# Whole stores for the last batch, and unread matmuls from the gather of batch 1 on, in a fused attention and mixture-of-depths kernel

## The chip, the cores and the metric

One core of a Trainium2 chip runs the kernel. The metric is device time in microseconds; the kernel before was run three times.

## The reference

Four batches of `x[6208, 256]` go through a cross-covariance attention over channels, and then through a mixture of depths that works on 128 tokens of each batch. Cut to what matters:

```python
qn = q / (norm(q, axis=1) + 1e-6)
kn = k / (norm(k, axis=1) + 1e-6)
a = softmax(kn.transpose(0, 2, 1) @ qn / tau)
x = v @ a

scores = x @ w_gate
out = x.copy()
for b in range(B):
    top = the 128 tokens of batch b with the largest scores
    xe = x[b, top]
    ye = relu(xe @ w1) @ w2
    out[b, top] = xe + sigmoid(scores[b, top])[:, None] * ye
```

q, k, v and out are float32, 25.4 MB each.

## The kernel before, in words

A batch is cut into six full chunks of 1024 rows and a remainder of 64 rows. In a full chunk each of the 128 partitions holds 8 neighbouring rows, so a partition's share of an output chunk is 8 KB of contiguous memory, and the chunk is 1 MB.

**Loads.** `emit_load` (L238, L240) issues the loads on POOL, which casts them to bf16 on the way: for each batch first q and k of all chunks, then v. `pump` emits them as far ahead as buffers and a limit of bytes in flight allow. In the model they share one ring (0), the stores another (1).

**First pass.** `p1_row` (L380 to L384) multiplies each row group of q and k into the sums of q-k products and of the norms, in PSUM. One chunk is 16 groups of three matmuls. `softmax_stages` makes the attention matrix of the batch from them.

**Second pass.** `p2_transpose` (L484) transposes v, `p2_score` (L529) makes the scores, `p2_out` (L563) multiplies by the attention matrix, and ScalarE copies the result to a staging tile (L574). When a chunk's staging tile is full, `out_store` calls `emit_store` (L586; L588 for the remainder), which issues the store on SP.

**Selection and the mixture of depths.** `select_stages` searches the threshold of the 128 largest scores, makes the indices, gathers the tokens' rows of v (L716, on POOL), and multiplies them by the attention matrix and by w1 and w2 (L740 to L800). `upd` (L804) is the result, and L818 scatters it into the output, on POOL, when every store of that batch has landed.

**The last batches.** L is batch 3 and E is batch 2. The stores of batches 2 and 3 wait until the last load, GATE, has landed. The last two chunks of batch 2 (`late`) are computed after all of batch 3, with the update added by matmuls (L570), so that the scatter of batch 2 need not wait for their stores; they are stored last of all. The scatter of batch 3 waits for the stores of batch 3 and not for those two. A full chunk of batch 3 is stored in two halves, partitions 0 to 63 and 64 to 127, issued one behind the other when the chunk is complete; all other chunks are stored whole.

**The order.** A loop at the end of the kernel writes the instructions in the order that a model gives: `Engines` holds a clock for each engine, `Rings` one for the transfers, and among the steps that are ready the loop takes the one of the smallest priority: chains of softmax and selection (0), scores (1), first pass and transposes (2), outputs (3). The model of PE knows two speeds, by how much PE did before. Where nothing is ready for more than FILL = 0.1 us, `unread` (L515) emits a matmul of constants into columns of the score bank that nobody reads; `cast_done`, true once the weights have been cast, allows it from early in batch 0 on. `gathered` is the set of batches whose gather has been emitted; with E = 2 it reaches that size at the gather of batch 1.

Of the kernel before, what the change touches and what calls it, by code (L numbers as in the profile page):

```python
# [17 lines left out]
P = 128  # L18
# [91 lines left out]
def kernel(  # L110
# [12 lines left out]
    nc = tc.nc  # L123
# [11 lines left out]
    NFULL = NL * CPL  # L135
# [34 lines left out]
    def lview(t, b, d):  # L170
        if d < NL:
            return t[b, d * LCH:(d + 1) * LCH, :].rearrange("(p s) c -> p s c", s=LR)
        return t[b, NL * LCH:N, :]

    def view(t, b, ci):
        if ci < NFULL:
            return lview(t, b, ci // CPL)[:, ci % CPL * RPP:(ci % CPL + 1) * RPP, :]
        return lview(t, b, NL)
# [4 lines left out]
    L = B - 1  # L183
    E = B - 2
# [8 lines left out]
    def late(b, ci):  # L193
        return b == E and ci in LATE
# [6 lines left out]
    def now():  # L201
        return eng.t["pe"]
# [49 lines left out]
    def pump():  # L252
        rings.run(now())
        flying[:] = [key for key in flying if rings.done.get(key, FAR) > now()]
        while nxt_unit[0] < len(units):
            u = units[nxt_unit[0]]
            if not slots[bucket(u)] or sum(length[key] for key in flying) >= AHEAD:
# [11 lines left out]
                      in_=moe_w1.rearrange("(dc p) f -> p dc f", p=P))  # L269
# [74 lines left out]
    gathered = set()  # L344
# [12 lines left out]
    def bank_free(kind):  # L357
        return banks[bank_pick(kind)][0]
# [154 lines left out]
    def unread():  # L513
        t = scores_of(sc_last[0])
        nc.tensor.matmul(t[:, 256:512], lhsT=ident_b, rhs=w1_sb[:, 0, 0:256], start=not sc_open[0],  # L515
                         stop=not sc_open[0])
        eng.pe(1, 256)
# [62 lines left out]
    def apart(later, earlier):  # L580
        tc.declare_no_dep(later.ins, earlier.ins, reason="rows of the last batch and of the batch before it")

    def emit_store(b, ci, lo, hi):
        st = stage_of[(b, ci)]
        if ci < NFULL:
            ins = nc.sync.dma_start(out=view(out, b, ci)[lo:hi], in_=st[lo:hi])  # L586
        else:
            ins = nc.sync.dma_start(out=view(out, b, ci), in_=st[:REM, 0, :])  # L588
        if late(b, ci):
            late_inst.append(ins)  # L590
            if L in scatter_inst:
                apart(ins, scatter_inst[L])
        return ins
# [278 lines left out]
    cast_done = False  # L872
    drained = False
    fill_at = [0.0]
    FILL = 0.1
# [3 lines left out]
    def stage_ready():  # L879
        if len(stage_keys) < ST_BUFS:  # L880
            return 0.0
        key = stage_keys[-ST_BUFS]
        if key in stage_free:
            return stage_free[key]
        return rings.landing(("st",) + key)

    def out_store(b, ci):
        dep = stage_done[(b, ci)]
        if b >= E and not gate_done:
            dep = max(dep, rings.landing(GATE))  # L890
        if late(b, ci):
            dep = max(dep, rings.landing(("scatter", E)))
        parts = (2 if b == L else 1) if ci < NFULL else 1
        for h in range(parts):
            key = ("st", b, ci) if h == parts - 1 else ("st", b, ci, h)
            issued = eng.issue("sp", 0.42, dep)
            rings.add(1, issued + 0.65, STORE / parts + 0.009 if ci < NFULL else 0.2, key, 0.45)
            ins = emit_store(b, ci, h * P // parts, (h + 1) * P // parts)
        stored[b].append(key)
        if not late(b, ci):  # L900
            held[b] -= 1
        return ins

    while True:
        pump()
        if not cast_done and now() > 8.0:
# [11 lines left out]
            cast_done = True  # L918
# [3 lines left out]
        if deferred and GATE in load_inst:  # L922
            for b, ci in deferred:
                st = out_store(b, ci)
                if not gate_done:
                    gate_done.append(1)
                    tc.add_manual_dep(
                        st.ins, load_inst[GATE].ins.name,
                        mybir.DependencyInfo(mybir.DependencyClass.Sync, mybir.DependencyReason.DATA),
                        reason="stores behind the last loads")  # L930
            deferred = []
        t = now()
# [3 lines left out]
        if eat_at < len(eat):  # L936
            kind, u, x = eat[eat_at]
            if u in loaded:
# [4 lines left out]
                r = rings.landing(arrival_key[u + (row,)]) + MARGIN  # L943
                if kind == "p1":
                    if u[2] == FIRST and x == 0:
                        r = max(r, acc_free[0])
                elif vt_slots or acc_dead[0] and u[2] < NL:
                    r = max(r, bank_free("vt"))
                else:
                    r = FAR  # L950
                able.append((r, 2, kind))
        if score_at < len(scores):
            b, g = scores[score_at]
            if b in aw_ready and (b, g) in vts:
                able.append((max(aw_ready[b], vt_ready[(b, g)]), 1, "S"))
        if out_at < len(outs):
            b, g, pr = outs[out_at]
            if b in a_ready and (b, g) in vts and score_at > gs.index(g) + b * len(gs):
                r = max(a_ready[b], vt_ready[(b, g)], bank_free("o"))
                if late(b, g[0]):  # L960
                    r = max(r, late_add[2] if E in scatter_inst else FAR)
                if g[0] < NFULL and g[1] == 0 and pr == 0:
                    r = max(r, stage_ready())
# [12 lines left out]
        if fit:  # L976
            r, prio, what = min(fit, key=lambda a: (a[1], a[0]))
        else:
            r, prio, what = min([a for a in able if a[0] > t], key=lambda a: (a[0], a[1]))
            if cast_done and r - t > FILL and t >= fill_at[0]:  # L980
                unread()
                fill_at[0] = now() + PAUSE
                continue
            if r - t > FILL and fill_at[0] > t:
                eng.t["pe"] = min(r, fill_at[0])
                continue
            eng.t["pe"] = max(t, r)
            t = now()
# [26 lines left out]
        elif what == "S":  # L1015
            b, g = scores[score_at]
            score_at += 1
            f = p2_score(b, g)
            if g == gs[-1]:
                chains.append(Chain(select_stages(b, f), b))  # L1020
        else:
            b, g, pr = outs[out_at]
            out_at += 1
            f = p2_out(b, g, pr)
            if out_at == len(outs) or outs[out_at][1] != g:
                vts.pop((b, g))
                if (b, g) in from_pool:
                    from_pool.discard((b, g))
                    vt_slots.append(f)
            if out_at == len(outs) or outs[out_at][1][0] != g[0]:  # L1030
                if b >= E and not gate_done:
                    deferred.append((b, g[0]))
                else:
                    out_store(b, g[0])
# [35 lines left out]
```

## Time and profile before

| what | us |
|---|---|
| median of 3 runs | 267.47 |
| lowest and highest | 266.99, 267.75 |
| the profiled execution | 267.31 |
| its span in the profile | 265.2 |
| PE busy | 231.5 (87%) |
| VectorE, ScalarE, POOL busy | 96.9, 100.4, 56.4 |
| chain that ended last: DMA, PE | 53%, 32% |

The profile comes from one execution, and times in it count from the start of its span. Busy time of PE overlaps itself, since matmuls are pipelined. PE is TensorE, DVE VectorE, ACT ScalarE, SP the engine that issues the stores, POOL GpSimd; L586 is line 586 of the kernel. "PEclk" is the share of TensorE's full clock that was granted. "[3.00 <-DMA x]" behind an instruction is the idle time of its engine before it and what ended most of it. Time to landing runs from a transfer's issue to its last byte.

### The profile page before, as it was taken

Reading aid. Unit: us, or ns where it says so; the run is one execution under the profiler, and the core shown is the slowest. Engines: PE = TensorE matmul, PEld = TensorE weight load, DVE = VectorE, ACT = ScalarE, POOL = GpSimd, SP = SyncE. Lnnn points to the kernel's source line nnn. Section 1 sums busy time; section 2 is a strip of 40 time slices with the busy share of each in tenths; the row PEclk is TensorE's granted clock in tenths of the full one; section 3 lists DMA queues with packets and bytes.
Section 4 is the critical chain, followed back from the end, with each engine's and each line's share of the span. In section 5 each row is a group of like instructions: output and inputs, shape, how many; then the busy total and the mean of one; then the engine's idle time right before and its main releaser. Section 6 shows DMA issues by size and latency. Waiting matters only on the chain.

```text
span 265.2 us, 7006 instructions
## 1 busy us (share of the span) xinstructions
PE 231.5 (87%) x3043; PEld 203.0 (77%) x3043; DVE 96.9 (37%) x410; ACT 100.4 (38%) x179; POOL 56.4 (21%) x105
## 2 busy tenths in 40 slices
PE   0099989999999979999999979999999989999660
PEld 0079878889889979798789969888989978787440
DVE  0100003567520013757630011747663287764030
ACT  3700004852830022854632002766122084597310
POOL 7223113212040105213021014133223300011001
PEclk9999999999999999999999999999999999999975
DMA  7999999999999999999999999999999997999994
GB/s 236 258 216 211 214 216 211 211 214 287 296 316 319 309 213 212 224 212 281 290 313 316 317 228 213 221 216 208 217 213 209 213 210 231 421 273 283 316 336 185
DMA packets 16847, 66.89 MB, mean 252 GB/s; under 512 B 2097, under 2 KB 3634, under 8 KB 13618
## 3 DMA queue, kind: packets, MB, share of 16 engines
q0 software_dynamic: 12528, 38.93, 73.6%
q1 hardware_dynamic: 4290, 27.53, 28.1%
q8 instruction: 23, 0.38, 0.5%
q14 instruction: 6, 0.05, 0.0%
HBM read 78.91 MB, written 25.95 MB: 395 GB/s over the span
## 4 chain that ended last, share of the span: by engine, by line
DMA 53%; PE 32%; issue 4%; DVE 3%; POOL 3%; ACT 1%; SPq 1%; POOLq 1%; DVEq 0%
DMA k_ch<-in_k_dram 39%; DMA v_ch<-in_v_dram 7%; PE s_ps L380 6%; PE o_ps L563 5%; DMA q_ch<-in_q_dram 5%; PE g_ps L384 3%; PE g_ps L382 3%; DMA out_dram<-stage 3%; PE vt_ps L484 3%; PE sc_ps L529 2%; PE sc_ps L515 1%; SPq L586 1%; PE g_ps L563 1%; PE m_ps L648 1%; PE s_ps L563 1%
## 5 line engine op out<-in xcount | busy, mean ns | idle before, releaser
L380 PE MATMUL s_ps<-q_ch,k_ch 128*128 128x256 bf16 x384 | 89.4, 277 | 17.7 <-DMA k_ch<-in_k_dram 17.7
L382 PE MATMUL g_ps<-q_ch 128*128 128x128 bf16 x384 | 85.1, 222 | 0.0
L384 PE MATMUL g_ps<-k_ch 128*128 128x128 bf16 x384 | 85.1, 222 | 0.0
L574 ACT COPY stage<-o_ps 128x512 f32<-128x512 f32 x80 | 45.3, 587 | 43.0 <-PE o_ps L563 40.3
L380 PEld LDWEIGHTS <-k_ch 128*128 128x128 bf16 x384 | 38.0, 99 | 20.0 <-DMA k_ch<-in_k_dram 19.1
L384 PEld LDWEIGHTS <-k_ch 128*128 128x128 bf16 x384 | 38.2, 99 | 5.0
L515 PE MATMUL sc_ps<-w_sb,ident_b 128*128 128x256 bf16 x293 | 41.7, 276 | 0.0
L563 PE MATMUL o_ps<-a_sb,vt_sb 128*128 128x256 bf16 (+1 forms) x278 | 40.1, 272 | 0.1
L382 PEld LDWEIGHTS <-q_ch 128*128 128x128 bf16 x384 | 38.1, 99 | 0.2
L563 PEld LDWEIGHTS <-vt_sb 128*128 128x128 bf16 (+1 forms) x296 | 26.7, 97 | 5.9 <-issue 1.6
L515 PEld LDWEIGHTS <-ident_b 128*128 128x128 bf16 x293 | 27.8, 99 | 3.5
L484 PE MATMUL vt_ps<-ident_b,v_ch 128*128 128x128 bf16 x360 | 25.3, 219 | 1.3 <-ACT vt_sb L498 1.2
L484 PEld LDWEIGHTS <-v_ch 128*128 128x128 bf16 x384 | 23.1, 97 | 2.9 <-issue 2.4
L238 POOL DMA_DIRECT2D v_ch<-in_v_dram x25 | 13.6, 545 | 38.1 <-DMA k_ch<-in_k_dram 22.0
L238 POOL DMA_DIRECT2D q_ch<-in_q_dram x25 | 13.9, 555 | 36.6 <-PE o_ps L563 6.4
L743 DVE COPY vgt<-vt_ps 128x256 bf16<-128x256 bf16 x4 | 1.2, 292 | 56.0 <-PE vt_ps L740 56.0
L399 DVE SCALAR_TENSOR_TENSOR junk<-g_ps,ident_f 128x128 f32<-128x128 f32 x16 | 4.7, 291 | 43.4 <-PE g_ps L384 42.9
L766 ACT COPY xe<-m_ps 128x256 f32<-128x256 f32 x4 | 1.5, 372 | 48.0 <-DVE awj L762 40.3
L498 ACT COPY vt_sb<-vt_ps 128x1024 bf16<-128x1024 bf16 (+1 forms) x22 | 18.0, 877 | 1.6 <-PE vt_ps L484 1.6
L630 DVE SCALAR_TENSOR_TENSOR cmp<-sc,wl,tab 128x392 bf16<-128x392 f32 x28 | 17.5, 626 | 1.0
L238 POOL DMA_DIRECT2D k_ch<-in_k_dram x25 | 13.7, 550 | 18.2 <-PE o_ps L563 5.9
L501 DVE COPY vt_sb<-vt_ps 128x1024 bf16<-128x1024 bf16 x18 | 12.2, 690 | 12.0 <-PE vt_ps L484 12.0
(165 smaller groups left out, 257.2 us busy)
## 6 DMA issues: line engine op xcount, KB each, us to landing
out_dram<-stage SPq DMA_DIRECT2D x18, 1024.0 KB, 11.1
q_ch<-in_q_dram POOLq DMA_DIRECT2D x23, 512.0 KB, 16.3
k_ch<-in_k_dram POOLq DMA_DIRECT2D x23, 512.0 KB, 18.3
v_ch<-in_v_dram POOLq DMA_DIRECT2D x23, 512.0 KB, 15.8
out_dram<-stage SPq DMA_DIRECT2D x12, 512.0 KB, 6.4
stage<-in_moe_w_dram SPq DMA_DIRECT2D x2, 1024.0 KB, 7.1
q_ch<-in_q_dram POOLq DMA_DIRECT2D x2, 256.0 KB, 16.0
k_ch<-in_k_dram POOLq DMA_DIRECT2D x2, 256.0 KB, 15.7
```

Source lines behind the costliest of these rows:

```text
L238: ins = nc.gpsimd.dma_start(out=t[:, rows, :], in_=lview(src, b, d)[:, rows, :])
L380: nc.tensor.matmul(s_ps[:, cc, :], lhsT=ks[:, sl], rhs=qs, start=begin and cc == 0, stop=end and cc == 1)
L382: nc.tensor.matmul(g_ps[:, cc, :], lhsT=qs[:, sl], rhs=qs[:, sl], start=begin and cc == 0, stop=False)
L384: nc.tensor.matmul(g_ps[:, 2 + cc, :], lhsT=ks[:, sl], rhs=ks[:, sl], start=False, stop=end and cc == 1)
L484: nc.tensor.transpose(vt_ps[:, cc, j, :parts], in_=vt[:parts, v0 + j, cc * P:(cc + 1) * P], identity=ident_b[:parts, :parts])
L498: nc.scalar.copy(vt_sb[:, :, :n, :parts], vt_ps[:, :, :n, :parts])
L501: nc.vector.tensor_copy(vt_sb[:, :, :n, :parts], vt_ps[:, :, :n, :parts])
L515: nc.tensor.matmul(t[:, 256:512], lhsT=ident_b, rhs=w1_sb[:, 0, 0:256], start=not sc_open[0], stop=not sc_open[0])
L529: nc.tensor.matmul(sc_ps[:parts, col, :], lhsT=vt_sb[:, cc, j, :parts], rhs=aw_sb[:, cc, :], start=cc == 0 and col == 0, stop=cc == 1 and ...
L563: nc.tensor.matmul(o_ps[:parts, pj, :], lhsT=vt_sb[:, cc, j, :parts], rhs=a_sb[:, cc, :], start=pj == 0 and cc == 0, stop=last and cc == 1 ...
L574: nc.scalar.copy(st[:parts, s0 + pair * 2:s0 + pair * 2 + m, :], o_ps[:parts, :m, :])
L630: nc.vector.scalar_tensor_tensor(out=cmp, in0=sc[:, :, None].to_broadcast([P, NCOL, NTHR]), scalar=wl[:, i, NTHR:NTHR + 1], in1=tab[:, Non ...
```

## The change

Chunks of batch 3 are stored in one part like all others. `emit_store` gets the index of the part and the number of parts, and takes every `parts`-th partition from `h` on; with one part that is all 128. The loop writes unread matmuls, and holds back PE's clock between two of them, only once two batches have had their gather emitted, in place of `cast_done`.

```diff
-    def emit_store(b, ci, lo, hi):
+    def emit_store(b, ci, h, parts):
         st = stage_of[(b, ci)]
         if ci < NFULL:
-            ins = nc.sync.dma_start(out=view(out, b, ci)[lo:hi], in_=st[lo:hi])
+            ins = nc.sync.dma_start(out=view(out, b, ci)[h:P:parts], in_=st[h:P:parts])
         else:
...
-        parts = (2 if b == L else 1) if ci < NFULL else 1
+        parts = 1
         for h in range(parts):
             key = ("st", b, ci) if h == parts - 1 else ("st", b, ci, h)
             issued = eng.issue("sp", 0.42, dep)
             rings.add(1, issued + 0.65, STORE / parts + 0.009 if ci < NFULL else 0.2, key, 0.45)
-            ins = emit_store(b, ci, h * P // parts, (h + 1) * P // parts)
+            ins = emit_store(b, ci, h, parts)
...
-            if cast_done and r - t > FILL and t >= fill_at[0]:
+            if len(gathered) >= E and r - t > FILL and t >= fill_at[0]:
                 unread()
                 fill_at[0] = now() + PAUSE
                 continue
-            if r - t > FILL and fill_at[0] > t:
+            if len(gathered) >= E and r - t > FILL and fill_at[0] > t:
                 eng.t["pe"] = min(r, fill_at[0])
                 continue
```

## Rows read from the trace of the kernel before

**Rows 1.** The page's slices, 6.63 us each: DMA busy share in tenths, and GB/s

```profile
DMA  7999999999999999999999999999999997999994
GB/s 236 258 216 211 214 216 211 211 214 287 296 316 319 309 213 212 224 212 281 290 313 316 317 228 213 221 216 208 217 213 209 213 210 231 421 273 283 316 336 185
```

**Rows 2.** The chain that ended last, in order of time: start, us, what

```profile
251.38 7.20 DMA out_dram<-stage
```

**Rows 3.** Busy time by stretch, from 227 us to 260 us

```profile
core 0: us, PE busy (x) PEld busy (x) DVE busy (x) ACT busy (x) POOL busy (x), PEclk, DMA share, GB/s
227.00:230.00 3.00, 2.93 (x30) 2.07 (x29) 1.97 (x9) 1.91 (x4) 0.00 (x0) 1.00 0.99 418
...
233.00:241.00 8.00, 8.00 (x100) 6.63 (x98) 5.37 (x23) 8.00 (x16) 1.15 (x1) 1.00 0.96 236
241.00:257.00 16.00, 12.11 (x106) 9.66 (x104) 3.82 (x16) 5.89 (x13) 0.99 (x1) 0.89 1.00 320
258.00:260.00 2.00, 0.00 (x0) 0.00 (x0) 0.00 (x0) 0.00 (x0) 0.29 (x1) 0.63 0.99 418
```

**Rows 4.** ScalarE's timeline: the last copies of batch 3 and of batch 2

```profile
240.46 0.58 ACT L574 COPY stage<-s_ps 128x512 f32<-128x512 f32 x1
...
248.35 0.58 ACT L574 COPY stage<-s_ps 128x512 f32<-128x512 f32 x1 [0.29 <-PE s_ps L570]
```

**Rows 5.** The timeline from 244 us: gather, first transpose, update and scatter of batch 3

```profile
244.10 0.99 POOL L716 DMA_INDIRECT vg<-in_v_dram,idx  x1 [6.72 <-DVE idx L710]
...
250.76 0.28 PE L740 MATMUL vt_ps<-ident_b,vg 128*128 128x128 bf16 x2 [2.45 <-DMA vg<-in_v_dram,idx]
...
256.23 0.48 DVE L804 SCALAR_TENSOR_TENSOR upd<-o_ps,gate,xe 128x256 f32<-128x256 f32 x1 [0.45 <-PE o_ps L800]
259.71 0.98 POOL L818 DMA_INDIRECT out_dram<-upd,idx  x1 [14.62 <-DMA out_dram<-stage]
```

**Rows 6.** The timeline of 95 to 101 us: the same steps of batch 0

```profile
95.39 0.28 PE L740 MATMUL vt_ps<-ident_b,vg 128*128 128x128 bf16 x2
...
100.15 0.48 DVE L804 SCALAR_TENSOR_TENSOR upd<-o_ps,gate,xe 128x256 f32<-128x256 f32 x1 [0.23 <-PE o_ps L800]
...
100.92 1.01 POOL L818 DMA_INDIRECT out_dram<-upd,idx  x1 [5.21 <-DVE upd L804]
```

**Rows 7.** DMA queues of 245 to 251 us (gather), and issues of 255 to 265

```profile
q0 software_dynamic: 144, 0.07, 9.0%
...
vg<-in_v_dram,idx POOLq DMA_INDIRECT x1, 6.6
...
out_dram<-upd,idx POOLq DMA_INDIRECT x1, 4.1
```

**Rows 8.** Busy time by stretch around the gather's landing (columns of rows 3)

```profile
248.40:250.70 2.30, 0.00 (x0) 0.00 (x0) 0.00 (x0) 0.54 (x1) 0.00 (x0) 1.00 1.05 371
...
251.50:255.00 3.50, 3.50 (x28) 2.98 (x28) 0.94 (x4) 1.06 (x3) 0.00 (x0) 0.53 0.96 311
```

**Rows 9.** Unread matmuls (L515) alone, by stretch: PE and PEld busy, PEclk, DMA, GB/s

```profile
0.00:137.30 137.30, 22.27 (x156) 14.70 (x156) 1.00 1.04 250
```

**Rows 10.** PE's timeline: first pass at 16.8 and at 22.1 us, unread matmuls

```profile
16.77 0.42 PE L380 MATMUL s_ps<-q_ch,k_ch 128*128 128x256 bf16 x1
...
17.20 0.42 PE L380 MATMUL s_ps<-q_ch,k_ch 128*128 128x256 bf16 x1
...
22.10 0.27 PE L380 MATMUL s_ps<-q_ch,k_ch 128*128 128x256 bf16 x1
...
22.32 0.27 PE L380 MATMUL s_ps<-q_ch,k_ch 128*128 128x256 bf16 x1
...
84.50 4.53 PE L515 MATMUL sc_ps<-w_sb,ident_b 128*128 128x256 bf16 x40
```

**Rows 11.** DMA issues of 101 to 104 us: count, KB each, median us to landing

```profile
v_ch<-in_v_dram POOLq DMA_DIRECT2D x2, 512.0 KB, 12.5
q_ch<-in_q_dram POOLq DMA_DIRECT2D x1, 512.0 KB, 16.0
```

## The prediction

> **What bounds the kernel now.** I read the slices of the page first: in 37 of the 40 the DMA engines are busy for 90% or more, while the bytes per second swing between about 210 and 420 GB/s [rows 1]. So the transfers bound the kernel, and what they deliver while "busy" differs. Next I read the end of the chain of waits: its last long piece is a transfer of `out_dram<-stage` that lands at 251.38 + 7.20 = 258.58 us [rows 2]. The profile's span ends at 265.2, so the end hangs on stores.
>
> Third came the stretches of the stores. While only the whole stores of batch 2 are queued, the engines move 418 GB/s. When the halves of batch 3 take over, they move 236 and then 320 GB/s at the same busy share (0.96 and 1.00), and when the last whole stores are left it is 418 again [rows 3]. That is the view on which the forecast rests: a store of 64 partitions keeps the 16 engines as busy and moves less.
>
> Is that a lack of work? The copies that fill the staging tiles say no. The last copy of batch 3 ends at 240.46 + 0.58 = 241.04, the last of the two chunks of batch 2 that come after it at 248.35 + 0.58 = 248.93 [rows 4], yet the last half lands only at 258.58. The stores have a backlog.
>
> Last I read who waits for them. The update of batch 3 is ready at 256.23 + 0.48 = 256.71, and its scatter starts at 259.71; the row names a store as the releaser [rows 5]. From there the span takes 265.2 - 259.71 = 5.49 us more.
>
> **The change part by part.** *Whole stores.* Twelve issues on SP become six; nothing else on SP changes, and the two late chunks were whole already. From 233.0 on the bytes left are six chunks of 1.049 MB, the remainder (0.066), two late chunks (2.10) and about 0.2 for scatter and gather. At 418 GB/s the stores of batch 3 need (6.29 + 0.07 + 0.2) / 0.418 = 15.7 us, to 248.7, and all of it (8.66 MB) 20.7 us, to 253.7. Both copies' ends (241.04, 248.93) are early enough. The wait of the scatter thus goes, and what is late next is the update at 256.71. In batch 0, where nothing held it, the scatter started 100.92 - 100.63 = 0.29 us after its update [rows 6]. So it starts at 257.00 instead of 259.71: **2.71 us** off. The late stores (253.7 and a landing) end before the scatter does, with nobody waiting for them.
>
> *The gather before it.* The update is the end of gather, MoE and update; its gather is issued at 244.10, in the middle of the halves, and lands 6.6 us later [rows 5, 7]. In 6 us its queue moved 144 packets, 9 per engine [rows 7]. If each waits for one 8 KB packet of a store on its engine, such a packet costs 8192 B / (320/16 GB/s) = 0.41 us among halves and 8192 / (418/16) = 0.31 us among whole stores: 9 x 0.10 = **0.9 us** less, which I take. The bounds: nothing, if the gather waits for other things; 2.5 us, if it gets as fast as the last scatter, 4.1 us from issue to landing beside little else [rows 7]. The value lies nearer to the lower end because store packets still stand beside it until 253.7.
>
> *The clock in the last MoE.* Between the last matmuls of the late chunks and the gather PE idles 2.3 us; the granted clock then falls from 1.00 to 0.53, towards the lower level, 1.2 GHz [rows 8]. The stretch from the first transpose to the update takes 256.71 - 250.76 = 5.95 us there, 100.63 - 95.39 = 5.24 at 2.4 GHz in batch 0 with other matmuls in between [rows 5, 6]. A shorter idle could give back 0.7 us, or nothing; I count nothing and keep both ends.
>
> *The unread matmuls.* 156 of them run before the gather of batch 1 at 137.3, 22.27 us of PE busy time [rows 9]; they go. They read constants and write columns that nobody reads, so no engine waits for them. What they carry is the clock. The longest run is 40 of them from 84.50, 4.5 us [rows 10]. Without them PE idles there, and rows 8 show a fall after 2.3 us. A chunk's first pass at 1.2 GHz costs twice as much: its 16 groups start 0.43 us apart at the kernel's start and 0.22 later [rows 10], so 16 x 0.21 = 3.4 us more per cold chunk. The cover is the transfers: loads issued in this stretch land 12.5 (v) to 16.0 us (q) later by the median of their kind [rows 11], so a first pass that is 3.4, or twice 3.4, us late still finds its loads queued, and DMA is busy for 90% or more there [rows 1]. I take **zero**; if that cover is gone, 3.4 us per cold chunk. On POOL the gather and scatter stand in line with the loads, and a later update holds the loads behind it by as much, under the same cover.
>
> The planner writes the order with its own clock, in which the fills no longer advance PE and a batch 3 store is one entry. Single groups of matmuls (0.44 us each) may change places; I take zero, and half a microsecond either way.
>
> Sum: 2.71 + 0.9 = 3.6 us. The profiled execution took 267.31 us, 2.1 more than its span, and is 0.16 below the median of the runs; from the median, 267.47 - 3.6 = **263.9 us**.
>
> A rule to set beside rows 3: the Trainium skill, "SBUF — State Buffer", section "Door 1: The DMA port swizzle", says that partitions 0 to 63 reach only 8 of the 16 ports, about 218 GB/s against 436 for all 128. The trace agrees on whole stores (418), and only in part on halves: 236 and 320, so neighbouring halves overlap. By the page alone rival 1 below would have no chance and the end would be the same, as the update sets it.
>
> **The rivals.** *1. The halves are not what is slow.* The low rate would belong to the tail (writes to memory, small packets beside them), and whole stores would run at it too. For it: 236 and 320 differ among themselves. Against it: 418 on both sides of the halves. It gives 267.5; chance 0.07.
>
> *2. The gather takes the place of the stores.* Behind larger stores it lands only when their queue is empty, at 253.7; the update follows 5.95 us later at 259.7, the scatter at 259.9 instead of 259.71: 267.7, no change. Against it: the gather landed at 250.7 with a backlog that lasted beyond 258. Chance 0.05.
>
> *3. The cold clock costs more than the tail gives (slower).* Place: the stretch from 84.5 to 104 us, and its like before. Two cold chunks in a row make the first pass of batch 1 6.8 us late, and softmax, update, scatter and the loads queued behind them on POOL with it. It decides from the point at which the lag, with what POOL adds, passes the 12.5 us of rows 11 and the transfers run dry; then up to 6.8 us are lost, and 6.8 - 3.6 = 3.2 remain: 270.7. For it: rows 8 and 10. Against it: rows 1 and 11. Chance 0.09. The Trainium skill, "TensorE: Matmul & The Clock Gate", section "HAM oscillation — how this bites in real kernels", describes its first half: waits for data between bursts let the gate close, and every burst starts cold. Rows 8 agree. By that page the chunks do run cold, which makes the matmuls late and by itself no transfer; if each wait added its cold burst to the time, as in that page's example, the end would be those 270.7.
>
> That the change does not do what it says I exclude: with one part the slice is all 128 partitions.
>
> **How the numbers follow.** The forecast has 0.79. Its own range: 2.71 + 2.5 + 0.7 = 5.9 us off at best, 261.6; at worst no gain in the gather, half a microsecond of order and half of lateness, 265.8. What is left out, 0.21, are the three rivals, so I hold the range at 261.4 to 266.0. A measurement of this kernel can tell about 0.3%, 0.8 us, from no change. Faster by more than that: 0.79; within it, rivals 1 and 2: 0.12; slower: 0.09.
>
> **What would show it.** Right: 400 GB/s or more from 233 until the stores are done, the last store of batch 3 landing near 250, the scatter released by the update and not by a store, the gather's landing below 6.6 us, no unread matmul before the gather of batch 1, and DMA still above 0.9 in the slices from 7 to 215 us. Cold first passes around 90 us at no cost would show the cover. Wrong: 300 GB/s again among whole stores (rival 1), a gather landing after 253 (rival 2), or DMA gaps between 85 and 125 us with the last load landing after 222 (rival 3).

## The result and the profile after

The changed kernel takes 265.38 us (median of 11 runs, 264.26 to 266.18) where the kernel before takes 267.75 beside it (11 runs, 266.56 to 269.67): a ratio of 0.9904 [0.9876, 0.9931]. That is 2.4 us off by the medians and 2.6 by the ratio. The forecast was 3.6 us off and 263.9; the time lies inside its range. The profiled execution took 265.91 us, with a span of 264.0 (before: 267.31 and 265.2), so these two executions differ by less than the medians do, by 1.2 us of span.

The stretches of the stores come first, as in [rows 3], with the same columns:

```profile
core 0: us, PE busy (x) PEld busy (x) DVE busy (x) ACT busy (x) POOL busy (x), PEclk, DMA share, GB/s
227.00:230.00 3.00, 2.92 (x25) 2.05 (x24) 2.24 (x10) 2.19 (x5) 0.00 (x0) 1.00 1.01 423
...
233.00:241.00 8.00, 8.00 (x101) 6.64 (x100) 5.16 (x24) 7.76 (x16) 1.01 (x1) 1.00 1.01 412
241.00:250.00 9.00, 5.79 (x57) 4.71 (x52) 1.29 (x6) 4.21 (x8) 1.01 (x1) 1.00 1.02 406
250.00:257.00 7.00, 4.50 (x29) 3.59 (x30) 1.06 (x4) 0.96 (x2) 0.00 (x0) 0.59 0.38 157
```

At the same busy share the engines move 412 and 406 GB/s, where halves moved 236 and 320. Then, from 250 on, DMA is mostly idle: the backlog is gone. The page's slices (6.6 us each, the rows of [rows 1]) show the same at the end. Up to there DMA is at nine tenths or more, but for the first slice and the one from 218 us, which stand at seven tenths before as well:

```profile
DMA  7999999999999999999999999999999997999932
GB/s 236 258 213 215 211 216 213 211 211 215 212 233 276 276 300 321 288 318 326 318 334 302 212 213 218 217 217 209 214 213 209 213 214 200 416 415 417 401 150 81
```

The chain of waits now has the last store of batch 3 as a piece that ends at 240.79 + 9.86 = 250.65 us, where [rows 2] had 258.58. The scatter, which has to wait for it, starts only at 260.22:

```profile
240.79 9.86 DMA out_dram<-stage
```

The steps of [rows 5] in the timeline after, with the last output matmuls and the last copy, which had no row there:

```profile
243.81 1.01 POOL L716 DMA_INDIRECT vg<-in_v_dram,idx  x1 [7.21 <-DVE idx L710]
...
252.50 0.40 PE L740 MATMUL vt_ps<-ident_b,vg 128*128 128x128 bf16 x2 [5.13 <-DMA vg<-in_v_dram,idx]
252.69 0.64 PE L563 MATMUL s_ps<-a_sb,vt_sb 128*128 128x256 bf16 x2
253.12 0.63 PE L570 MATMUL s_ps<-d_b,late_oh 128*128 128x256 bf16 x2
253.55 0.63 PE L563 MATMUL s_ps<-a_sb,vt_sb 128*128 128x256 bf16 x2
253.97 0.64 PE L570 MATMUL s_ps<-d_b,late_oh 128*128 128x256 bf16 x2
...
254.64 0.59 ACT L574 COPY stage<-s_ps 128x512 f32<-128x512 f32 x1 [6.87 <-PE s_ps L570]
...
259.46 0.48 DVE L804 SCALAR_TENSOR_TENSOR upd<-o_ps,gate,xe 128x256 f32<-128x256 f32 x1 [0.45 <-PE o_ps L800]
260.22 0.98 POOL L818 DMA_INDIRECT out_dram<-upd,idx  x1 [15.41 <-DVE upd L804]
```

The scatter's releaser has changed from a store to the update, as forecast. But the gather takes 2.1 us longer to land than before (8.7 us from its issue, not 6.6), and behind the first transpose stand eight output matmuls that ran ahead of it before. Their copy ends at 255.23 instead of 248.93 [rows 4]. The issues of 238 to 262 us (KB each, median us to landing) give the landings:

```profile
out_dram<-stage SPq DMA_DIRECT2D x4, 1024.0 KB, 8.8
vg<-in_v_dram,idx POOLq DMA_INDIRECT x1, 8.7
out_dram<-upd,idx POOLq DMA_INDIRECT x1, 2.4
```

The clock around the longer wait, as in [rows 8]:

```profile
251.00:254.00 3.00, 1.50 (x9) 1.13 (x10) 0.29 (x1) 0.00 (x0) 0.00 (x0) 0.53 0.24 94
254.00:258.00 4.00, 4.00 (x30) 3.43 (x29) 0.76 (x3) 1.65 (x4) 0.00 (x0) 0.50 0.51 215
```

A granted clock of 0.50 is the lower level, 1.2 GHz: the last MoE (the mixture of depths) runs cold. The account from one profiled span to the other, each term a difference of the rows above and [rows 5]:

| Term | before, us | after, us | difference |
|---|---|---|---|
| gather issued at | 244.10 | 243.81 | -0.29 |
| gather issued to first transpose | 6.66 | 8.69 | +2.03 |
| first transpose to the update's end | 5.95 | 7.44 | +1.49 |
| update's end to scatter | 3.00 | 0.28 | -2.72 |
| scatter to the end of the span | 5.49 | 3.78 | -1.71 |
| sum | 265.2 | 264.0 | -1.20 |

So 4.4 us were gained behind the update and 3.5 lost ahead of it. The experiments ask where each of the four terms comes from. Their kernels compute all that the reference asks; where unread matmuls are added or left out, only unread columns differ.

### The profile page after: what moved, and what is told of

It is laid out like the page before. It is cut to its first block, busy times and chain, and to the rows that moved or that the text cites. A ratio compares the mean times of both kernels' runs of the same rounds, so it can differ in the third digit from the quotient of the medians.

```text
span 264.0 us, 6650 instructions
## 1 busy us (share of the span) xinstructions
PE 218.4 (83%) x2867; PEld 189.2 (72%) x2867; DVE 97.9 (37%) x412; ACT 97.0 (37%) x177; POOL 56.4 (21%) x105
## 4 chain that ended last, share of the span: by engine, by line
DMA 40%; PE 37%; ACT 9%; issue 7%; DVE 4%; POOL 2%; POOLq 1%; DVEq 0%; ACTq 0%
DMA k_ch<-in_k_dram 24%; PE o_ps L563 8%; DMA v_ch<-in_v_dram 7%; PE s_ps L380 7%; ACT stage L574 6%; DMA q_ch<-in_q_dram 5%; PE vt_ps L484 4%; DMA out_dram<-stage 4%; PE g_ps L384 4%; PE g_ps L382 4%; PE sc_ps L529 3%; PE sc_ps L515 2%; ACT vt_sb L498 1%; PE o_ps L800 1%; DVE junk L399 1%
## 5 line engine op out<-in xcount | busy, mean ns | idle before, releaser
L563 PEld LDWEIGHTS <-vt_sb 128*128 128x128 bf16 (+1 forms) x296 | 27.3, 99 | 9.2 <-issue 5.6
L484 PE MATMUL vt_ps<-ident_b,v_ch 128*128 128x128 bf16 x360 | 26.1, 223 | 2.6 <-ACT vt_sb L498 2.6
L484 PEld LDWEIGHTS <-v_ch 128*128 128x128 bf16 x384 | 24.0, 100 | 3.8 <-issue 2.3
L399 DVE SCALAR_TENSOR_TENSOR junk<-g_ps,ident_f 128x128 f32<-128x128 f32 x16 | 4.7, 291 | 57.8 <-PE g_ps L384 57.3
L238 POOL DMA_DIRECT2D v_ch<-in_v_dram x25 | 13.6, 548 | 30.7 <-DMA k_ch<-in_k_dram 18.7
L515 PE MATMUL sc_ps<-w_sb,ident_b 128*128 128x256 bf16 x117 | 19.4, 306 | 0.4 <-DVE sc L601 0.4
L238 POOL DMA_DIRECT2D k_ch<-in_k_dram x25 | 13.6, 543 | 28.5 <-PE o_ps L563 7.0
L501 DVE COPY vt_sb<-vt_ps 128x1024 bf16<-128x1024 bf16 x20 | 13.3, 689 | 16.5 <-PE vt_ps L484 16.5
L394 ACT COPY s_sb<-s_ps 128x512 f32<-128x512 f32 x4 | 2.3, 587 | 39.3 <-PE s_ps L380 39.3
L498 ACT COPY vt_sb<-vt_ps 128x1024 bf16<-128x1024 bf16 (+1 forms) x20 | 16.4, 866 | 1.0 <-PE vt_ps L484 1.0
L818 POOL DMA_INDIRECT out_dram<-upd,idx x4 | 4.0, 1006 | 58.6 <-DVE gej L657 26.1
```

The source lines that it names most:

```text
L238: ins = nc.gpsimd.dma_start(out=t[:, rows, :], in_=lview(src, b, d)[:, rows, :])
L484: nc.tensor.transpose(vt_ps[:, cc, j, :parts], in_=vt[:parts, v0 + j, cc * P:(cc + 1) * P], identity=ident_b[:parts, :parts])
L498: nc.scalar.copy(vt_sb[:, :, :n, :parts], vt_ps[:, :, :n, :parts])
L501: nc.vector.tensor_copy(vt_sb[:, :, :n, :parts], vt_ps[:, :, :n, :parts])
L563: nc.tensor.matmul(o_ps[:parts, pj, :], lhsT=vt_sb[:, cc, j, :parts], rhs=a_sb[:, cc, :], start=pj == 0 and cc == 0, stop=last and cc == 1 ...
```

## The experiments

**e1: whole stores alone.** The kernel before with

```diff
-        parts = (2 if b == L else 1) if ci < NFULL else 1
+        parts = 1
```

> Whole stores alone, the unread matmuls as before. Theory (the whole gain is in the stores of batch 3): about 265.4 us, as with the full change; 400 GB/s or more from 233 us on, the gather of batch 3 landing some 8.7 us after its issue, and the last pair of output matmuls standing behind the wait for the gather. Rival (the fewer unread matmuls in the first half carry part of the gain): 266.5 to 267.5 us.

Measured: 265.78 us (12 runs) against 267.48 (28 runs, shared by e1 to e4), 0.9931 [0.9896, 0.9966]. The stores run at

```profile
233.00:241.00 8.00, 8.00 (x100) 6.63 (x99) 5.40 (x21) 8.00 (x17) 1.01 (x1) 1.00 1.01 413
```

and the scatter is released by the update. So most of the gain is this one part. The gather did not take the 8.7 us that were expected: its first transpose comes 6.92 us after its issue. The profiled execution is the fastest of the twelve (263.85 us), and PE's clock stays up in its last MoE, though PE idled 3.36 us ahead of it:

```profile
250.00:257.00 7.00, 4.32 (x46) 3.25 (x46) 1.97 (x7) 1.56 (x4) 0.00 (x0) 1.00 0.61 248
```

With the last pair of output matmuls behind the first transpose as in the changed kernel, the steps from there to the update's end take 5.10 us here (252.57 to 257.67) and 7.44 there, at a granted clock of 0.63 over them.

In the written order of instructions e1 differs from the kernel before on PE at one place only: the last pair of output matmuls stands behind the gather's first transpose. The store entries in the planner's model moved it; the unread matmuls have no part in it.

**e2: the later unread matmuls alone.** The kernel before with

```diff
-            if cast_done and r - t > FILL and t >= fill_at[0]:
+            if len(gathered) >= E and r - t > FILL and t >= fill_at[0]:
...
-            if r - t > FILL and fill_at[0] > t:
+            if len(gathered) >= E and r - t > FILL and fill_at[0] > t:
```

> Unread matmuls only from the gather of batch 1 on, batch 3 stored in halves as before. Theory: no change, 267.0 to 268.2 us, the first store behind the last load again at 222.0 us, 240 to 330 GB/s among the halves. Rival (the unread matmuls cost or gave something): 266 us or less, or 269 us or more, with the first store of batch 2's rest at another time than 222.0.

Measured: 266.15 us (12 runs), 0.9958 [0.9926, 0.999]: 1.3 us less, where none was expected; the rival's 266 or less was not reached either. The profiled execution (267.01 us) is 0.9 above the median, so its trace cannot show where the 1.3 us come from. The halves are as slow as before, and the scatter waits for one of them:

```profile
233.00:241.00 8.00, 8.00 (x102) 6.75 (x101) 5.02 (x23) 7.61 (x16) 1.25 (x1) 1.00 0.99 254
...
259.63 0.98 POOL L818 DMA_INDIRECT out_dram<-upd,idx  x1 [15.02 <-DMA out_dram<-stage]
```

**e3: the last output pair ahead of the wait.** The changed kernel with an edit in the planner that lets the last gather's consumer come only when all outputs are written:

```diff
             if self.need[0] == "dma":
+                if self.b == L and out_at < len(outs):
+                    return FAR
                 return rings.landing(self.need[1]) if calm(self.b) else FAR
```

> The full change, and the chain of batch 3 takes the gathered rows only after the last output matmuls are written, which puts the last pair of the late chunk in front of the wait on PE again. Theory (the pair cost the last mixture of depths 1.5 us of its 7.4): about 263.9 us, first transpose to update in 5.9 us, last store issued by 249.5 instead of 255.3, gather landing still 8 to 9 us after its issue. Rival (the pair only filled time in which PE had to wait anyway): 265.4 us, unchanged.

Measured: 264.91 us (11 runs), 0.991 [0.988, 0.994]. In its timeline:

```profile
244.88 1.00 POOL L716 DMA_INDIRECT vg<-in_v_dram,idx  x1 [7.81 <-DVE idx L710]
...
253.00 0.40 PE L740 MATMUL vt_ps<-ident_b,vg 128*128 128x128 bf16 x2 [3.90 <-DMA vg<-in_v_dram,idx]
...
258.32 0.48 DVE L804 SCALAR_TENSOR_TENSOR upd<-o_ps,gate,xe 128x256 f32<-128x256 f32 x1 [0.45 <-PE o_ps L800]
```

From the first transpose to the update's end are now 5.80 us, 1.64 less than 7.44: the pair's place explains that term of the account, together with the clock, which is granted at 0.63 over that stretch in the changed kernel and at 0.73 from 253.0 to 258.8 us here. The median gained only 0.5, inside the interval and between the two times expected; this profile's gather was issued 1.07 us later. The gather still took 8.1 us, so its lateness has another cause than the order. It landed while the stores still moved:

```profile
252.00:254.00 2.00, 1.00 (x7) 0.82 (x8) 0.29 (x1) 0.00 (x0) 0.00 (x0) 0.68 0.90 381
```

**e4: halves again, but of every second partition.** The changed kernel with the old count of parts; `emit_store` then takes `h:P:2`, 64 partitions spread over all:

```diff
-        parts = 1
+        parts = (2 if b == L else 1) if ci < NFULL else 1
```

> The full change, but batch 3's chunks again in two parts of 64 partitions, every second partition instead of the first and the last 64; the order on PE is that of the kernel with halves. Theory (what was slow is the block of 64 neighbouring partitions): 400 GB/s or more, as with whole stores, and with 4 instead of 8 pieces of a store per engine in front of it the gather lands sooner than behind whole stores, about 6.6 us after its issue: 262 to 263 us. Rival (what was slow is the size, half a megabyte per store): 240 to 330 GB/s and 267 to 268 us, like the halves.

Measured: 262.78 us (6 runs), 0.9801 [0.9741, 0.9861]: 2.6 us below the changed kernel. Stretches and landing (issues of 243.8 to 246.8 us):

```profile
233.00:241.00 8.00, 8.00 (x100) 6.53 (x98) 5.26 (x22) 7.92 (x16) 1.01 (x1) 1.00 0.99 398
241.00:250.00 9.00, 7.46 (x72) 6.21 (x69) 2.01 (x12) 5.55 (x11) 1.00 (x1) 1.00 1.01 396
```

```profile
vg<-in_v_dram,idx POOLq DMA_INDIRECT x1, 6.4
```

A store of 64 partitions and 512 KB is not slow in itself: 398 GB/s against 236 and 254 for the same size in neighbouring partitions. What was slow is the block of neighbours. With smaller pieces the gather lands after 6.4 us, and the written order has the pair ahead of the wait again. Both lost terms of the account shrink at once, and the gained ones stay. Against e2 only the choice of the 64 partitions differs, and PE's matmuls run in the same order in both traces: 266.15 and 262.78 us.

**e5: e4 with the unread matmuls of before.**

```diff
-            if len(gathered) >= E and r - t > FILL and t >= fill_at[0]:
+            if cast_done and r - t > FILL and t >= fill_at[0]:
...
-            if len(gathered) >= E and r - t > FILL and fill_at[0] > t:
+            if r - t > FILL and fill_at[0] > t:
```

> Batch 3 in two striped parts as in the run before, and the unread matmuls from early in batch 0 on, as in the kernel before: against the kernel before only the choice of the 64 partitions differs. With the other runs this makes the third pair that differs in the early unread matmuls alone. Theory (they change nothing that a measurement shows): 262.3 to 263.5 us, as with striped parts and late unread matmuls (262.8). Rival (they cost about 1 us, as the pair with halves, 267.5 and 266.15, says): 263.8 us or more.

Measured: 263.56 us (6 runs), 0.9874 [0.9816, 0.9932] against 267.23 (11 runs, shared by e5 to e8): 0.8 above e4, just above the theory's range and short of the rival's 263.8, so it decides neither. But against the kernel before only the choice of partitions differs, and PE's matmuls run in the same order in both traces: 3.7 us off by the medians, and 347 and 410 GB/s from 233 to 241 and from 241 to 250 us where the kernel before has 236 and 319. Its profiled execution had the whole tail late, with the gather issued at 247.31.

**e6: quarters, every fourth partition.** The changed kernel with

```diff
-        parts = 1
+        parts = (4 if b == L or late(b, ci) else 1) if ci < NFULL else 1
```

> The full change, batch 3 and the two late chunks in four striped parts of 32 partitions; the order that the planner writes puts the last pair behind the wait for the gather again. Theory (the gather waits for whole pieces of stores on each engine, so smaller pieces let it through): it lands 5 to 5.6 us after its issue, from 6.4 with half pieces and 8.1 to 8.7 with whole stores; the pair behind the wait costs 1.5 us in the mixture of depths, as with the full change. Rival (it waits for the bytes in the queue): 6.4 us or more.

Measured, a single run: 260.91 us. The stores slow a little (366 GB/s in 233 to 241 us), but the first transpose comes 4.45 us after the gather's issue, at 249.38, sooner than either expectation. The pair behind it did not cost the 1.5 us expected: from there to the update's end are 5.10 us, at a granted clock of 1.00 from 249 to 255 us, against 4.77 with the pair ahead (e9 and e10 below).

**e7: e4 with a warm PE in the last wait.** The planner is told that the last gather takes longer, so that it writes unread matmuls into the wait:

```diff
-        rings.add(0, issued + 1.6, 0.5, ("gather", b), 0.1)
+        rings.add(0, issued + 1.6, 0.5, ("gather", b), 4.0 if b == L else 0.1)
```

> Batch 3 in two striped parts, and the planner told that the gather of batch 3 lands 3.9 us later, so that it writes 18 more unread matmuls in front of the wait for it. Theory (PE idles 2.4 us there and the clock of the last mixture of depths falls to 1.2 GHz): granted clock 1.00 instead of 0.5 to 0.76 in the stretch of the last mixture of depths, first transpose to update in 5.1 to 5.3 us instead of 6.0, 262.0 us. Rival (the clock does not matter there, as waits between engines set the pace): 262.8 us, unchanged.

Measured: 261.26 us (6 runs), 0.9786 [0.9736, 0.9837]. The median is 1.5 below e4's, but the two intervals overlap, and e4's runs go from 260.50 to 263.67. The stretch of the last MoE, e4's first and then that of e7:

```profile
252.00:257.00 5.00, 4.63 (x36) 3.56 (x35) 1.88 (x7) 1.06 (x3) 0.00 (x0) 0.69 0.51 216
```

```profile
250.00:255.00 5.00, 4.39 (x46) 3.01 (x43) 2.38 (x8) 0.97 (x3) 0.00 (x0) 1.00 0.85 359
```

At a granted clock of 1.00 the steps from the first transpose (250.31) to the update's end (255.07) take 4.76 us; e4, at 0.69, took 6.05 (251.23 to 257.28). So the clock is worth 1.3 us in that stretch. That the unread matmuls hold it up is not shown by this pair alone: e5 has none in that wait, PE idled 2.04 us there, and its steps took 4.77 us at 1.00 as well.

**e8: e4 with no unread matmul before the gather of batch 2.** `len(gathered) >= E` becomes `len(gathered) >= L` in both conditions:

```diff
-            if len(gathered) >= E and r - t > FILL and t >= fill_at[0]:
+            if len(gathered) >= L and r - t > FILL and t >= fill_at[0]:
...
-            if len(gathered) >= E and r - t > FILL and fill_at[0] > t:
+            if len(gathered) >= L and r - t > FILL and fill_at[0] > t:
```

> Batch 3 in two striped parts, and unread matmuls only from the gather of batch 2 on: those of the batches 1 and 2 go as well. Theory (transfers bound the kernel until 222 us, so the clock there is free): 262.3 to 263.5 us, the first store behind the last load at 222.0 us again. Rivals: 261.8 us or less, if each unread matmul in the first 200 us costs something; 264 us or more, if the clock in the last first pass, from 180 to 212 us, sets the start of the tail.

Measured: 262.76 us (6 runs), 0.9834 [0.9772, 0.9897], e4's 262.78 again. The unread matmuls alone (L515, columns of [rows 9]):

```profile
77.00:165.00 88.00, 0.00 (x0) 0.00 (x0) 0.94 1.05 284
```

The clock falls a little (0.94 from 77 to 165 us), and the first store behind the loads is issued at 221.97, where the changed kernel has 222.03. The time is the same with what PE loses there, so the loss costs nothing that a run shows. The order of the last MoE is not e4's, though: the last copy of batch 2 comes behind the gather (254.21 us, 249.07 in e4), and the first transpose to the update's end takes 6.80 us.

**e9 and e10: quarters with the pair ahead.** Both are the changed kernel with e3's edit. e9 has e6's count of parts; in e10 only the chunks stored last (named in `LATE`) of batches 2 and 3 are quartered:

```diff
-        parts = 1
+        parts = 4 if b >= E and ci in LATE else 1
```

> Four striped parts of 32 partitions for batch 3 and the two late chunks, as in the run with quarters, and the last pair of output matmuls in front of the wait for the gather again. Theory: gather 4.4 to 4.6 us after its issue as there, last store 1.5 us earlier, mixture of depths in 5.0 us or less; 259.5 to 260.5 us. Rival (the pair is hidden in the wait): 260.9 us.

> As the run before it in this call, but only the last two chunks of batch 3 and the two late chunks are stored in quarters, all others whole. Theory (what the gather waits for is the size of the pieces that are in the queue when it is issued, and quarters themselves move somewhat fewer bytes): gather again 4.4 to 5 us after its issue, 400 GB/s or more from 233 to 241 us where the quarters had 366; 259.5 to 260.5 us, the same or a little less than with quarters throughout. Rival (pieces queued long before count as well): 6 us or more.

Measured: e9 261.35 us, 0.9761 [0.9717, 0.9804]; e10 260.78 us, 0.9756 [0.971, 0.9802] (6 runs each, against 267.68, 13 runs, shared with e11). The two cannot be told apart, and both beat the kernel before and the changed one. Both missed the 259.5 to 260.5 us expected, and e9 is above its rival's 260.9 too. The issues beside the gather, e9 (243 to 245.2 us) and then e10 (the same):

```profile
out_dram<-stage SPq DMA_DIRECT2D x3, 256.0 KB, 3.9
vg<-in_v_dram,idx POOLq DMA_INDIRECT x1, 4.1
```

```profile
out_dram<-stage SPq DMA_DIRECT2D x2, 256.0 KB, 6.2
vg<-in_v_dram,idx POOLq DMA_INDIRECT x1, 5.8
```

e9 gets its gather soonest, but its stores slow beside it (366 and 348 GB/s in 233 to 241 and 241 to 250 us); e10 keeps 411 and 391. Of e9's stores 0.99 MB are still to move when its scatter starts at 254.17, of e10's 0.13: e9's scatter lands after 3.9 us, and the span runs on for 5.33 us, where e10 takes 2.4 and 3.89. In both the last MoE has a clock of 1.00 with no unread matmul added for it: first transpose to the update's end is 4.77 us in either. PE idled less than before ahead of it (hardly in e9, 1.60 us in e10), but idle time alone does not say what clock follows: e1 has 1.00 after 3.36 us, and e2 0.76 from 250 to 257 us after 1.92.

**e11: the unread matmuls back, the order kept.** The changed kernel with 84 unread matmuls written into the waits before the gather of batch 1, and the planner's clocks set back after each, so that the written order stays that of the changed kernel but for them:

```diff
+            if len(gathered) < E and cast_done and r - t > FILL:
+                kept, eng.t["pe"] = dict(eng.t), t
+                clock = (eng.win, eng.load, eng.full)
+                while eng.t["pe"] + 0.2 < r:
+                    unread()
+                    eng.t["pe"] += PAUSE
+                eng.t.update(kept)
+                eng.win, eng.load, eng.full = clock
```

> The full change, and 84 unread matmuls put back into the waits ahead of the gather of batch 1 without a word to the planner, so that all other instructions keep the order of the full change. Theory (what the early unread matmuls cost, 0.4 to 1.3 us in three pairs, is the order that the planner wrote with them, not the matmuls): 265.4 us, norms of batch 1 at 90.6 us and of batch 2 at 165 to 166.5 us as with the full change. Rival (the matmuls themselves cost): 265.8 us or more, and the norms later; or they give something by keeping the clock: 264.9 us or less.

Measured: 265.4 us (8 runs), 0.9907 [0.9872, 0.9942], the changed kernel's time. Up to 137 us its trace has 105 unread matmuls where the changed kernel has 15:

```profile
0.00:137.00 137.00, 15.31 (x105) 9.66 (x106) 0.99 1.04 256
```

Neither they nor the clock that they hold up (0.99 against 0.97) change the time. That the small gain of e2 belongs to the order that the planner writes without them follows by elimination and is not shown by itself.

## Why the prediction was right, and where it was off

**Rows 3 and the scatter's wait: right, and the size too.** The forecast said 400 GB/s or more, the last store of batch 3 landing near 250, the scatter released by its update, 2.71 us off. Measured: 412 and 406, 250.65, and the wait fell from 3.00 to 0.28 us, 2.72 off. Rival 1 falls. What is slow is narrower than I put it: e4 and e5 show that neither the size nor the count of partitions is slow, but their being neighbours. The rule that the prediction set beside rows 3, from the Trainium skill, "SBUF — State Buffer", section "Door 1: The DMA port swizzle", bears on this: partitions 0 to 63 reach half of the ports. The traces agree in kind: stripes, which touch both blocks, ran at 398, blocks at 236 and 254. No run shows the ports themselves.

**The gather: the step that failed.** I put it 0.9 us sooner, by the time of one store packet ahead of each of its nine on an engine, with bounds of 0 and 2.5 sooner. It came 2.0 us later, outside the bounds; later was left out of them without a reason and stood only in rival 2, at 0.05. What the runs show in its place is that the gather lands about when the stores issued beside it land, and that this takes longer the more bytes of stores are queued at its issue. Queued are the bytes that the stores' queue moves from then on, less the stores issued later. For e9 and e10, from the gather's issue to the end (packets, MB, share; then the stores issued):

```profile
q1 hardware_dynamic: 773, 4.18, 69.3%
out_dram<-stage SPq DMA_DIRECT2D x15, 256.0 KB, 3.3
```

```profile
q1 hardware_dynamic: 802, 4.34, 71.4%
out_dram<-stage SPq DMA_DIRECT2D x12, 256.0 KB, 3.7
```

That leaves 0.25 and 1.20 MB, a store of 256 KB being 0.262 MB.

| Kernel | Pieces beside the gather, KB | Queued at its issue, MB | Their landing, us | Gather issued to first transpose, us |
|---|---|---|---|---|
| changed kernel | 1024 | 2.05 | 8.2 | 8.69 |
| e11 | 1024 | 1.67 | 7.5 | 8.21 |
| e3 | 1024 | 1.57 | 7.0 | 8.12 |
| e1 | 1024 | 1.59 | 6.9 | 6.92 |
| before | 512, neighbours | 0.52 | 6.7 | 6.66 |
| e2 | 512, neighbours | 0.52 | 6.7 | 6.14 |
| e8 | 512, stripes | 1.20 | 7.6 (a store of 1024) | 6.64 |
| e4 | 512, stripes | 1.23 | 7.2 (a store of 1024) | 6.41 |
| e7 | 512, stripes | 0.96 | 7.0 | 6.35 |
| e5 | 512, stripes | 0.73 | 6.0 | 6.26 |
| e10 | 256 | 1.20 | 5.9 | 5.81 |
| e6 | 256 | 0.36 | 4.0 | 4.45 |
| e9 | 256 | 0.25 | 3.7 | 4.18 |

The bytes per second do not order the last column (236 to 413 GB/s, all between 4 and 9 us). Rival 2, the gather in place of the stores, was thus half right in its mechanism and wrong in its form: the gather does wait behind stores, but not for an empty queue (381 GB/s were moving when e3's landed). Bytes queued count by themselves: e9 and e10 have the same size of piece, and with 0.95 MB more queued the gather of e10 takes 1.63 us longer. The size of the piece seems to count too, by less: at 1.2 MB queued it is 5.81 us with 256 KB and 6.41 or 6.64 with 512. These are single profiles, and e1 and the two kernels with neighbouring halves do not fit by bytes alone.

**The planner's order: the second term that was mis-sized.** I took 0, and half a microsecond either way, for single groups of matmuls that change places. The last output pair behind the gather costs 7.44 - 5.80 = 1.64 us of the last MoE where the clock is low (e3), and 5.10 - 4.77 = 0.33 us at a clock of 1.00 (e6 against e9 and e10). In the median the pair's place is worth 0.5 us, which the intervals do not separate from nothing. A far larger move is told under the unread matmuls below.

**What made up for it.** The forecast let the span run on for the same 5.49 us after the scatter. It ran 3.78: with an empty queue the scatter landed after 2.4 us, not 4.1 [rows 7]. This term, -1.71, stood nowhere in the sum; the row was read only as a bound for the gather. Had I read the backlog's end at 250 to its consequence, the same row would have given it. The other profiles bear it out: the span runs on for 3.8 to 3.9 us after the scatter's start in the nine with at most 0.35 MB of stores still to move by then, for 4.23 us with 0.48 MB (e6), and for 5.3 to 5.5 us with 0.52 to 0.99 MB (before, e2, e9).

**The clock in the last MoE.** I counted zero out of 0 to 0.7. The wait grew instead of shrinking, so nothing came back, and zero was right for the wrong reason. Its worth was under-bounded: the stretch takes 1.3 us less at 1.00 in e7 than in e4, and with the pair behind the gather 2.3 us less in e1 (5.10) than in the changed kernel (7.44).

**The unread matmuls: zero was right, its mechanism was not met.** Zero was taken with the transfers as cover for a first pass that runs cold, and up to 6.8 us late, from 84.5 us on. No such pass is in the trace: the granted clock is 1.00 from 84 to 104 us, and the first pass of batch 1 is done 13.6 us sooner. Its first norm, before and then after:

```profile
104.57 0.29 DVE L399 SCALAR_TENSOR_TENSOR junk<-g_ps,ident_f 128x128 f32<-128x128 f32 x1 [3.93 <-PE g_ps L384]
90.94 0.29 DVE L399 SCALAR_TENSOR_TENSOR junk<-g_ps,ident_f 128x128 f32<-128x128 f32 x1 [14.35 <-PE g_ps L384]
```

The planner now writes that pass ahead of work on batch 0, whose scatter moves from 100.92 [rows 6] to 118.43 us. That is no change of place of single groups, and it was not foreseen. The clock falls elsewhere, to 0.59 from 132 to 140 us, at no cost that the time shows. The price of a cold chunk was read at the kernel's start [rows 10], where the granted clock is 1.00 (14 to 24 us), so the clock is not shown to be the reason there. The output matmuls above do show the doubling: pairs start 0.43 us apart at 0.50 (252.69 and 253.12 us) and 0.22 apart at 1.00 (246.12 and 246.34). e11 and e8 agree: neither adding 84 nor leaving out more changes the time, and DMA stays at nine tenths or more. Rival 3 falls by the time, without its cold chunks having been put to the test. With it falls the rule from the Trainium skill, "TensorE: Matmul & The Clock Gate", section "HAM oscillation — how this bites in real kernels", by which each wait's cold burst adds to the time, as a rule for this kernel: the clock does fall, and the time does not follow. The order that goes with the unread matmuls gave 1.3 us on halves (e2), 0.8 on stripes (e5 to e4) and 0.4 on whole stores (e1 to the changed kernel), of which only the first has an interval that leaves out zero. Which move in the order does it was not isolated.

The sum came out near the forecast, 2.6 for 3.6, because two errors of opposite sign in part made up for each other: 3.5 us lost ahead of the update where 0.9 was to be gained, and 1.7 found behind the scatter. (The two profiled executions alone differ by 1.2 us.) That the total came so near is luck; the term of rows 3 is not.

## What to carry to other kernels

In this kernel a store of some partitions was fast with every second or fourth one (398 and 366 GB/s) and slow with a block of neighbours (236), and the GB/s of a stretch at a full DMA share show which it is. A small transfer on which everything waits lands about when the large ones issued beside it do, so keep little queued when it is issued, and cut the large ones that stand beside it into small striped pieces. Here e10, with only those cut, takes 260.78 us, and e3, which differs from it in the parts alone, 264.91. When a backlog goes, look at each later transfer that stood in it and not only at the one that waited for it, and read the written order again after any edit to a planner's costs.

## What the runs showed that was not expected

The tail is a chain of nearly fixed length. From the first norm of batch 3 (L399) to the token indices (L710) it takes 31.8 to 32.2 us in all thirteen profiles: 211.57 to 243.38 in the changed kernel, 213.42 to 245.22 in e1, 215.06 to 246.88 in e5.

```profile
211.57 0.29 DVE L399 SCALAR_TENSOR_TENSOR junk<-g_ps,ident_f 128x128 f32<-128x128 f32 x1
...
243.38 0.15 DVE L710 TENSOR_SCALAR idx<-tok 128x1 int32<-128x1 f32 x1
```

Its start varied by 4.0 us between profiled executions (211.02 in e8 to 215.06 in e5). In e5 the granted clock had dipped ahead of it:

```profile
152.00:172.00 20.00, 17.71 (x205) 15.53 (x203) 5.61 (x26) 5.21 (x9) 5.26 (x9) 0.91 1.07 222
172.00:215.00 43.00, 42.44 (x611) 38.58 (x610) 21.29 (x87) 14.31 (x27) 11.68 (x21) 0.96 1.08 212
```

The changed kernel has 1.00 in both stretches. In e5 the first store behind the loads is issued at 221.99 as elsewhere, and yet the gather comes 3.5 us later than in the changed kernel. So between 152 and 215 us a full DMA share is no cover for this chain: PE is busy for 42.4 of the last 43 us, and lateness there shows at the end. The dip is not the cause everywhere. e8, the earliest, has 0.96 from 172 to 215 us as well, and e3, e4, e6, e9 and e11 start at 212.5 to 212.8 with 1.00 in both stretches. What sets the start was not tried. It is one reason why single profiles of these kernels differ by a microsecond or two, and why the medians carry the verdicts.
